# Four row transposes issued together, weight steps begun earlier, two products moved ahead of the last mixing

## The chip, the cores and the metric

One core of a Trainium2 chip runs the whole program. The metric is the device time of one execution in microseconds; of the kernel before there are three runs. The engines carry short names: PE is TensorE (PEld its weight loads), DVE is VectorE, ACT is ScalarE, POOL is GpSimd and SP is SyncE, which here only issues DMAs. SPq is SP's queue of DMA issues.

## The reference

Three stages follow one another. Gated linear attention over 4 batches, 8 heads, 768 positions and head size 48; a dense block on the 3072 tokens; a mixture of 8 experts in which each token goes to two.

```python
state = alpha[t][:, None] * state + outer(k[t], v[t]);  y[t] = q[t] @ state     # per batch and head
h = (x @ w1) * (x @ w2) @ w3;  x = h @ w_out                                     # 384 -> 1024 -> 384
top2 of x @ w_gate + log1p(exp(x @ w_noise)) * noise;  two weights by softmax
out[rows of expert e] += weight * (relu(x[rows] @ ew1[e]) @ ew2[e])              # 384 -> 1024 -> 384
```

## The kernel before, in words

**Chunks and groups.** Attention goes in 24 chunks of 128 tokens (j = 0 to 23). For each chunk PE runs `scores` (L293), `mix` (L326: four products of the queries with the running state `Zs`, L332, and 24 products of scores and values, L343), `state` (L354: the update of `Zs`, whose products are read and scaled on DVE at L386 and L387) and `xturn` (L389: six small transposes of the chunk's result). Three chunks are one group of 384 tokens (g = 0 to 7). The dense block runs by groups: 16 `wide` products per group (L516, nine matmuls each), then six `narrow` halves (L539, twelve matmuls each), then `finish` and `route` on DVE and ACT (L559, L597), which leave the two experts of each token and a one-hot count `M`. `rank` (L644) turns `M` into places in a table of tokens with two small matmuls (L650, L651), some DVE work, and six indirect DMAs on POOL. The rank of the last group is run inside `experts`.

**Who sets the order.** The order on PE is written by hand. `att_units` (L692) yields the attention steps with a planned cost each, `mix_units` (L790) the dense steps. After each attention step, as many dense steps are put behind it as the planned costs allow: the sum of dense costs may be 1.9 times the attention cost beyond 60. With these costs nothing is put between `xturn(22)` and `mix(23)`, the last mixing; four `wide` products of group 6, a rank and one `narrow` half stand between `mix(23)` and `xturn(23)`. When attention is over, the rest of `mix_units` follows, and after each unit of cost above zero `prepare(n)` (L1021) issues n steps of the list `todo`, with n from the tuple `EARLY`. On DVE, ACT, POOL and SP the order is chosen by the scheduler of the framework from the order in the program and from readiness, except that a step of `todo` stands behind the last DVE and ACT instructions issued so far, and that the DMAs sent through `queued` (L819) keep their order on each engine.

**Weights of an expert.** `expert_weights` (L830) gives two lists of steps: `a` for the first matrix (13 steps) and `b` for the second (11). In each: 0 and 1 load its halves (`get`, L856, 768 KB each, into one of three buffers `es`); 2 and 3 take the greatest absolute value of a half (DVE, L859; the second one ends in `em`, L862); 4 is empty; 5 is `over_all`, a PE matmul of one column (L867) that waits for `em`; 6 is `scales`; from 7 on the halves are cut into a high and a low f16 part (`eh` on ACT, L174, and `el` on DVE, L178), six cuts for `a`, four for `b`. A fourth half can be loaded when a buffer is free again, thus after the cuts of an earlier half.

**Experts.** An expert has 832 rows in two parts, 512 and 320. `fetch_part` loads the row numbers (`mt`, SP) and gathers the rows by indirect DMA (POOL, `xg`); `turn_part` (L966) transposes 128 rows by DMA into `xT` (SP, L894). Part 0 of all experts has one `xT` buffer. `first(e, p, f)` is one product of the first layer (L900 to L902, nine matmuls, evicted by ACT at L903 and DVE at L904), eight to a part; `second(e, p, t)` (L910 to L912, 24 matmuls) ends in a `put` of 128 rows (ACT L933, POOL L934). Expert 0's part 0 is followed by expert 1's part 0, then part 1 of both.

In `experts` before, expert 1's weight steps begin after the last `narrow` half. Its list has 24 entries, five of them empty: one is issued after each of the eight `first(0, 0, f)`, three after each `second(0, 0, t)`, one after each `first(1, 0, f)`. `rank(7)` comes after the eight `first`. Each of expert 1's four row transposes is issued ahead of its own `second(0, 0, t)`; the row numbers and gathers of expert 0's part 1 come after the first `second`.

Of the kernel before, what the change touches and what calls it, by code (L numbers as in the profile page):

```python
# [29 lines left out]
TG = G // P  # L30
NG = NTOK // G
# [22 lines left out]
RATIO = 2.0  # L54
TK = 60
R2 = 1.9
EARLY = (0, 3, 0, 3, 2, 1, 0, 1, 0, 1, 0, 1, 0, 1, 0, 0, 0, 0, 2, 0, 1, 1, 1, 1, 0, 0, 0, 0)
PGL = range(4)
NPC = 4
PB = 512  # L60
# [18 lines left out]
def body(ctx, tc, q, k, v, alpha, mw1, mw2, mw3, mwo, wg, wn, noise, ew1, ew2, out, dbg=None):  # L79
# [309 lines left out]
    def xturn(j):  # L389
        ys = YS.pop(j)  # L390
        if j % TG == 0:
            XT[j // TG] = xp.tile([P, 2 * NK, G], F16, name="xT")
        xt = bank(2 * NK, P, dt=F16)
        for kk in range(2 * NK):
            nc.tensor.transpose(xt[:, kk, :], ys[:, kk // NK, kk % NK * P:(kk % NK + 1) * P], ident16)
        nc.scalar.activation(XT[j // TG][:, :, j % TG * P:(j % TG + 1) * P], xt, AF.Copy)  # L396
# [292 lines left out]
    def unit(c, f, *a):  # L689
        return c, (lambda: f(*a))  # L690

    def att_units():  # L692
        yield unit(0.0, prep_open, 0)
        for pr in range(NP):
            yield unit(0.33, prep_decay, 0, pr)
            if pr:
                yield unit(0.66, prep_qk, 0, pr - 1)
        yield unit(0.66, prep_qk, 0, NP - 1)
        yield unit(1.7, scores, 0)
        yield unit(0.44, ktok, 0)  # L700
        yield unit(1.7, scores, 1)
        yield unit(2.55, mix, 0)
        yield unit(0.44, ktok, 1)
        yield unit(0.75, state, 0)
        yield 0.34, (lambda: (xturn(0), done.add(0)))
        yield unit(0.0, loads_of_1)
        yield unit(1.7, scores, 2)
        yield unit(2.55, mix, 1)
        yield unit(0.44, ktok, 2)
        yield unit(0.75, state, 1)  # L710
        yield 0.34, (lambda: (xturn(1), done.add(1)))
        yield unit(0.0, prep_open, 1)
        yield unit(0.0, norms, 1)
        yield unit(0.33, prep_decay, 1, 0)
        yield unit(2.55, mix, 2)
        yield unit(0.33, prep_decay, 1, 1)
        yield 0.34, (lambda: (xturn(2), done.add(2)))
        yield unit(0.66, prep_qk, 1, 0)
        yield unit(0.33, prep_decay, 1, 2)
        yield unit(0.66, prep_qk, 1, 1)  # L720
        yield unit(0.33, prep_decay, 1, 3)
        yield unit(0.66, prep_qk, 1, 2)
        yield unit(0.66, prep_qk, 1, 3)
        yield unit(0.0, scales_of, 1)
        yield unit(0.0, load, 2)
        yield unit(0.0, tables)
        yield unit(0.75, state, 2)
        yield unit(1.7, scores, 3)
        yield unit(0.44, ktok, 3)
        for j in range(TG, NG * TG):  # L730
            st, cc = divmod(j, TG)
            more = st + 1 < NG
            if j + 1 < NG * TG:
                yield unit(1.7, scores, j + 1)
            if more and cc == 0:
                yield unit(0.0, prep_open, st + 1)
                yield unit(0.0, norms, st + 1)
                yield unit(0.33, prep_decay, st + 1, 0)
                yield unit(0.33, prep_decay, st + 1, 1)
            yield unit(2.55, mix, j)  # L740
            if more and cc == 0:
                yield unit(0.66, prep_qk, st + 1, 0)
                yield unit(0.33, prep_decay, st + 1, 2)
            if more and cc == 1:
                yield unit(0.66, prep_qk, st + 1, 2)
            if j + 1 < NG * TG:
                yield unit(0.44, ktok, j + 1)
            yield unit(0.75, state, j)
            if more and cc == 0:
                yield unit(0.66, prep_qk, st + 1, 1)  # L750
                yield unit(0.33, prep_decay, st + 1, 3)
            if more and cc == 1:
                yield unit(0.66, prep_qk, st + 1, 3)
                yield unit(0.0, scales_of, st + 1)
                if st + 2 < NG:
                    yield unit(0.0, load, st + 2)
            yield 0.34, (lambda j=j: (xturn(j), done.add(j)))

    def fuse_units():

# [192 lines left out]
    NTP = [-(-(c1 - c0) // P) for c0, c1 in PARTS]  # L953
    EW, EX, EH, WV = {}, {}, {}, {}
    adds = {}
    todo = []

    def fetch_part(e, p):
        c0, c1 = PARTS[p]
        t0, nt = c0 // P, -(-(c1 - c0) // P)  # L960
        rows = P + NTOK - (NL * G if e < NFR and p == 0 else 0)
        mt = slots(table[e, :, t0:t0 + nt, :], nt, p)
        xT = ep.tile([P, 2 * NK, nt * P], F16, name=f"xT{p}", bufs=1)
        EX[e, p] = (mt, xT, [gather(mt, t, rows) for t in range(nt)])

    def turn_part(e, p, t):  # L966
        mt, xT, xg = EX[e, p]
        turn(xg[t], xT, t)
# [29 lines left out]
    def open_experts():  # L998
        nonlocal ep
        ep = ctx.enter_context(tc.tile_pool(name="ep", bufs=2, side="right", reuse_waits="tile"))  # L1000
        assert NG - NL not in RT and NG - NL - 1 not in RT
        a, b = weights_for(0)
        todo.extend(a[2:4] + b[2:3] + a[5:10] + b[1:2] + a[10:] + b[3:4] + b[5:])
        for e in range(NFR):
            fetch_part(e, 0)

    def weights_for(e):

        EW[e], a, b = expert_weights(e)
        for get in a[:2] + b[:1]:  # L1010
            get()
        return a, b

    def pause(n):
        return [lambda: None] * n
# [5 lines left out]
    def prepare(n):  # L1021

        if not n or not todo:
            return
        with ExitStack() as st:
            for e in (mybir.EngineType.DVE, mybir.EngineType.Activation):
                for i in [i for i in nc.cur_bb.bb.instructions[-60:] if i.engine == e][-1:]:
                    st.enter_context(tc.issue_after(i))
            for _ in range(min(n, len(todo))):
                todo.pop(0)()  # L1030

    def experts():
        prepare(len(todo))
        a, b = weights_for(1)
        todo.extend(pause(1) + a[2:4] + pause(1) + a[5:11] + b[1:2] + a[11:] + b[2:3] + pause(2) + b[3:4] + pause(1) + b[5:])
        for f in range(NF):
            first(0, 0, f)
            prepare(1)
        rank(NG - 1)
        for t in range(NTP[0]):  # L1040
            turn_part(1, 0, t)
            second(0, 0, t)
            prepare(3)
            if t == 0:
                fetch_part(0, 1)
        for f in range(NF):
            first(1, 0, f)
            prepare(1)
            if 0 < f <= NTP[1]:
                turn_part(0, 1, f - 1)  # L1050
        prepare(len(todo))
        fetch_part(1, 1)
        next_weights(2)
        for f in range(NF):
            first(0, 1, f)
            prepare(f // 4)
        for t in range(NTP[1] - 1):
            turn_part(1, 1, t)
            second(0, 1, t)
            prepare(2)  # L1060
        turn_part(1, 1, NTP[1] - 1)
        rest = last_few(0)
        li = overflow_plan()
        for e in range(1, E):
            if e > 1:
                for f in range(NF):
                    first(e, 0, f)
                    if f == 0:
                        rest()
                    prepare(1)  # L1070
            if e + 1 < E:
                fetch_part(e + 1, 0)
            for f in range(NF):
                first(e, 1, f)
                if f == 0 and e == 1:
                    rest()
                prepare(1)
            if e + 1 < E:
                fetch_part(e + 1, 1)
            for t in range(NTP[0]):  # L1080
                second(e, 0, t)
                prepare(2)
                if e + 1 < E:
                    turn_part(e + 1, 0, t)
            prepare(len(todo))
            if e + 2 < E:
                next_weights(e + 2)
            if e < E - 1:
                for t in range(NTP[1] - 1):
                    turn_part(e + 1, 1, t)  # L1090
                    second(e, 1, t)
                turn_part(e + 1, 1, NTP[1] - 1)
                rest = last_few(e)
        second(E - 1, 1, 0)
        rest = last_few(E - 1)
        second(E - 1, 1, 1, rest)
        return li
# [65 lines left out]
    done, ready = set(), set()  # L1163
# [3 lines left out]
    with tc.manual_schedule(engines={mybir.EngineType.PE}):  # L1167
# [4 lines left out]
        for c, f in att_units():  # L1172
# [16 lines left out]
            while nxt is not None and nxt[2] in ready | {0} and tm < RATIO * (min(ta, TK) - t0) + R2 * max(ta - TK, 0.0):  # L1189
                nxt[1]()  # L1190
                tm += nxt[0]
                nxt = next(M, None)
        att.close()
        open_experts()
        early = iter(EARLY)
        while nxt is not None:
# [38 lines left out]
```

## Time and profile before

| | us |
|---|---|
| median of three runs | 972.02 |
| lowest, highest | 971.38, 975.17 |
| the profiled execution itself | 978.31 |
| its span (first to last instruction) | 976.6 |
| PE busy | 924.2 (95%) |
| DVE, ACT, POOL busy | 616.1, 457.8, 254.0 |

The profiled execution is 6.29 us above the median of the runs; 1.71 us of it lie outside the span. Times in the rows are counted from the start of the span. In a row of a timeline stand start, duration, engine, line, operation, destination and sources, shapes, how often, and in square brackets the idle time of the engine before it with what ended it. A row that covers several instructions runs from the first start to the last end.

### The profile page before, as it was taken

The numbers are of one execution on the slowest core, as the hardware profiler recorded it, in microseconds if no ns is written. First come the engines' busy times: TensorE is split into PE (matmuls) and PEld (weight loads), VectorE is DVE, ScalarE is ACT, GpSimd is POOL, SyncE is SP. The second block draws the span as 40 slices with busy tenths as digits, with TensorE's granted clock in tenths as the row PEclk, the third lists the DMA queues.
The fourth block names the chain that finished last, engine by engine and source line by source line (L and its number), as shares of the span: only waits on it lengthen the run. The fifth ranks groups of instructions, "written<-read, shape, count | busy, mean of one in ns | idle before, by whom it ended". The sixth has DMA issues, their size and how long they took to land. (4 is left out here: it accounts for less than half of the span.)

```text
span 976.6 us, 17652 instructions
## 1 busy us (share of the span) xinstructions
PE 924.2 (95%) x6823; PEld 607.8 (62%) x6823; DVE 616.1 (63%) x1697; ACT 457.8 (47%) x916; POOL 254.0 (26%) x246
## 2 busy tenths in 40 slices
PE   7889999999899998999999989999999999999996
PEld 4777777777666675666655445654656565656564
DVE  6698878576778697686768736626354454545320
ACT  3876665363565746555446424324243343334321
POOL 1121110004041311204052061433333333333313
PEclk9798899999999999999999989999999999999998
DMA  9886571334805224000234264874658575656313
GB/s 242 224 163 109 162 195 53 63 52 145 187 3 96 27 66 58 25 2 26 68 102 127 87 129 139 138 174 104 167 89 163 102 178 118 161 124 157 41 13 46
DMA packets 189269, 105.54 MB, mean 108 GB/s; under 512 B 156912, under 2 KB 174912, under 8 KB 189184
## 3 DMA queue, kind: packets, MB, share of 16 engines
q1 hardware_dynamic: 172624, 68.04, 31.5%
q0 software_dynamic: 16560, 36.37, 17.3%
q8 instruction: 54, 0.88, 0.4%
q14 instruction: 31, 0.25, 0.1%
HBM read 73.06 MB, written 20.31 MB: 96 GB/s over the span
## 5 line engine op out<-in xcount | busy, mean ns | idle before, releaser
L904 DVE SCALAR_TENSOR_TENSOR hl<-ps,hh 128x512 f16<-128x512 f32 (+1 forms) x128 | 74.9, 587 | 110.9 <-ACT hh L903 110.9
L934 POOL DMA_INDIRECT out_dram<-ysb,mt x56 | 88.3, 1576 | 210.3 <-ACT ysb L933 91.3
L900 PE MATMUL ps<-xT,eh 128*128 128x320 f16 (+1 forms) x384 | 132.0, 344 | 4.5 <-DMA xT<-xg 4.5
L901 PE MATMUL ps<-xT,eh 128*128 128x320 f16 (+1 forms) x384 | 131.9, 344 | 0.0
L902 PE MATMUL ps<-xT,el 128*128 128x320 f16 (+1 forms) x384 | 131.7, 343 | 0.0
L912 PE MATMUL ps<-eh,hl 128*128 128x384 f16 x384 | 125.2, 326 | 0.0
L911 PE MATMUL ps<-el,hh 128*128 128x384 f16 x384 | 125.2, 326 | 0.0
L910 PE MATMUL ps<-eh,hh 128*128 128x384 f16 x384 | 125.2, 326 | 0.0
L903 ACT ACTIVATE hh<-ps 128x512 f16<-128x512 f32 (+1 forms) x128 | 65.9, 516 | 113.6 <-PE ps L902 112.5
L933 ACT ACTIVATE ysb<-ps,wv 128x384 f32<-128x384 f32 (+1 forms) x56 | 32.5, 580 | 151.9 <-PE ps L912 75.2
L178 DVE SCALAR_TENSOR_TENSOR el<-es,esc,eh 128x512 f16<-128x512 f32 (+1 forms) x80 | 67.0, 856 | 46.4 <-ACT eh L174 45.1
L679 POOL DMA_INDIRECT table<-md,ad x48 | 49.3, 1028 | 162.7 <-DVE ad L676 130.4
L888 POOL DMA_INDIRECT xg<-x2s,mt x56 | 56.4, 1008 | 57.8 <-DMA mt<-table 37.6
L176 POOL TENSOR_TENSOR sm<-sf,sm 128x512 f16<-128x512 f32 x24 | 28.4, 1203 | 161.1 <-ACT sm L174 161.1
L529 ACT ACTIVATE ab<-ps 128x384 f32<-128x384 f32 (+2 forms) x136 | 61.4, 465 | 17.0 <-PE ps L527 15.5
L525 PE MATMUL ps<-xT,w1h 128*128 128x384 f16 (+2 forms) x204 | 65.7, 323 | 2.0 <-ACT ab L529 1.5
L525 PE MATMUL ps<-xT,w0h 128*128 128x384 f16 (+2 forms) x204 | 65.4, 322 | 1.1 <-ACT xT L396 1.1
L549 PE MATMUL ps<-Wh,gh 128*128 128x400 f16 x192 | 63.9, 333 | 2.2 <-ACT gh L174 2.2
L527 PE MATMUL ps<-xT,w1l 128*128 128x384 f16 (+2 forms) x204 | 65.8, 323 | 0.0
L526 PE MATMUL ps<-xT,w1h 128*128 128x384 f16 (+2 forms) x204 | 65.7, 323 | 0.0
L526 PE MATMUL ps<-xT,w0h 128*128 128x384 f16 (+2 forms) x204 | 65.4, 322 | 0.0
L527 PE MATMUL ps<-xT,w0l 128*128 128x384 f16 (+2 forms) x204 | 65.3, 321 | 0.0
(285 smaller groups left out, 2080.6 us busy)
## 6 DMA issues: line engine op xcount, KB each, us to landing
es<-in_moe_w_dram SPq DMA_DIRECT2D x32, 768.0 KB, 4.8
s<-in_moe_w_dram POOLq DMA_DIRECT2D x16, 512.0 KB, 4.3
out_dram<-zero POOLq DMA_DIRECT2D x5, 960.0 KB, 9.4
v<-in_v_dram SPq DMA_DIRECT2D x24, 192.0 KB, 3.6
x2s<-xr SPq DMA_DIRECT2D x24, 192.0 KB, 1.9
pad<-in_alpha_dram SPq DMA_DIRECT2D x21, 192.0 KB, 4.3
pad<-in_q_dram SPq DMA_DIRECT2D x21, 192.0 KB, 4.8
pad<-in_k_dram SPq DMA_DIRECT2D x21, 192.0 KB, 5.0
```

The lines of the kernel that those rows point to most:

```text
L178: nc.vector.scalar_tensor_tensor(lo, src, scale, hi, op0=OP.mult, op1=OP.subtract)
L525: nc.tensor.matmul(pm, wab[i][0][:, kk, fs], xT[:, kk, cs], start=kk == 0, stop=False)
L526: nc.tensor.matmul(pm, wab[i][0][:, kk, fs], xT[:, NK + kk, cs], start=False, stop=False)
L527: nc.tensor.matmul(pm, wab[i][1][:, kk, fs], xT[:, kk, cs], start=False, stop=kk == NK - 1)
L900: nc.tensor.matmul(pm, w1h[:, kk, fs], xT[:, kk, :n], start=kk == 0, stop=False)
L901: nc.tensor.matmul(pm, w1h[:, kk, fs], xT[:, NK + kk, :n], start=False, stop=False)
L902: nc.tensor.matmul(pm, w1l[:, kk, fs], xT[:, kk, :n], start=False, stop=kk == NK - 1)
L904: nc.vector.scalar_tensor_tensor(hl[:, f], pm, 0.0, hh[:, f], op0=OP.max, op1=OP.subtract)
L910: nc.tensor.matmul(py[:n], hh[:, f, ts], w2h[:, f], start=f == 0, stop=False)
L911: nc.tensor.matmul(py[:n], hh[:, f, ts], w2l[:, f], start=False, stop=False)
L912: nc.tensor.matmul(py[:n], hl[:, f, ts], w2h[:, f], start=False, stop=f == NF - 1)
L934: i = queued(lambda: nc.gpsimd.indirect_dma_start(out=out, out_offset=bass.IndirectOffsetOnAxis(ap=mt[:n, t, 0:1].bitcast(U32), axis=0), i ...
```

## The change

Four things change. The planned cost of `mix(23)` falls by 1.6 and that of `xturn(22)` rises by 1.6, so two `wide` products and `rank(5)` are put between them. In `EARLY`, three steps of expert 0 are issued one or two units sooner, after `narrow(6, 2, 0)`, and two steps of expert 1 are issued after `narrow(7, 1, 0)` and `narrow(7, 2, 0)`. Expert 1's list has no empty entries, and the load of the second half of its second matrix, `b[1]`, stands ahead of the cuts. In `experts`, the four transposes are issued together, ahead of `rank(7)`, and two steps in place of three follow each `second(0, 0, t)`. The number of matmuls, cuts, loads and transposes stays the same.

```diff
-EARLY = (0, 3, 0, 3, 2, 1, 0, 1, 0, 1, 0, 1, 0, 1, 0, 0, 0, 0, 2, 0, 1, 1, 1, 1, 0, 0, 0, 0)
+MH = 1.6
+EARLY = (0, 3, 0, 6, 0, 0, 0, 1, 0, 1, 0, 1, 0, 1, 0, 0, 0, 0, 2, 0, 1, 1, 1, 1, 1, 0, 1, 0)
...
-            yield unit(2.55, mix, j)
+            yield unit(2.55 - (MH if j == NG * TG - 1 else 0.0), mix, j)
...
-            yield 0.34, (lambda j=j: (xturn(j), done.add(j)))
+            late_on = MH if j == NG * TG - 2 else 0.0
+            yield 0.34 + late_on, (lambda j=j: (xturn(j), done.add(j)))
...
+        todo.append(first_of_1)
+
+    def first_of_1():
+        a, b = weights_for(1)
+        todo.extend(a[2:4] + a[5:7] + [b[1]] + a[7:11] + [b[2]] + a[11:] + b[3:4] + b[5:])
+        todo.pop(0)()
...
     def experts():
-        prepare(len(todo))
-        a, b = weights_for(1)
-        todo.extend(pause(1) + a[2:4] + pause(1) + a[5:11] + b[1:2] + a[11:] + b[2:3] + pause(2) + b[3:4] + pause(1) + b[5:])
         for f in range(NF):
             first(0, 0, f)
-            prepare(1)
+            prepare((0, 1, 1, 1, 1, 1, 1, 1)[f])
+        for t in range(NTP[0]):
+            turn_part(1, 0, t)
         rank(NG - 1)
         for t in range(NTP[0]):
-            turn_part(1, 0, t)
             second(0, 0, t)
-            prepare(3)
+            prepare(2)
             if t == 0:
                 fetch_part(0, 1)
```

## Rows read from the trace of the kernel before

**Rows 1.** The profile page, busy time and share of PE.

```profile
PE 924.2 (95%) x6823; PEld 607.8 (62%) x6823; DVE 616.1 (63%) x1697; ACT 457.8 (47%) x916; POOL 254.0 (26%) x246
```

**Rows 2.** Waits of PE from 470 to 600 us: total, times, longest.

```profile
PE ps L900 <- DMA xT<-xg: 4.5, 1, 4.5
PE ps L867 <- DVE em L862: 3.2, 2, 1.6
PE ps L332 <- DVE Zs L387: 2.0, 1, 2.0
PE ps L651 <- DVE M L640: 0.5, 1, 0.5
```

**Rows 3.** Waits of PE from 600 us to the end.

```profile
PE ps L867 <- DVE em L862: 3.2, 5, 2.4
```

**Rows 4.** Timeline of PE about the last two mixings.

```profile
470.50 1.03 PE L332 MATMUL ps<-Zs,Qt 112*128 112x96 f32 x8
...
473.44 0.33 PE L525 MATMUL ps<-xT,w0h 128*128 128x384 f16 x1
...
482.56 1.57 PE L332 MATMUL ps<-Zs,Qt 112*128 112x96 f32 x8 [2.00 <-DVE Zs L387]
...
487.12 0.33 PE L525 MATMUL ps<-xT,w1h 128*128 128x384 f16 x1
```

**Rows 5.** Windows: length, busy PE, PEld, DVE, ACT, POOL, granted clock, DMA, GB/s.

```profile
484.00:486.00 2.00, 2.00 (x29) 1.48 (x28) 0.38 (x4) 0.58 (x2) 0.00 (x0) 0.50 0.41 33
544.00:559.00 15.00, 13.40 (x64) 5.90 (x63) 14.55 (x63) 5.63 (x12) 0.00 (x0) 1.00 0.11 40
580.00:582.00 2.00, 2.00 (x5) 0.66 (x6) 0.00 (x0) 0.00 (x0) 1.70 (x2) 0.50 1.07 176
```

**Rows 6.** Timeline of DVE about the last two mixings.

```profile
476.73 0.62 DVE L178 SCALAR_TENSOR_TENSOR ys<-ps,xsc,ys 128x384 f16<-128x384 f32 x1 [0.65 <-ACT ys L174]
...
481.67 0.74 DVE L387 TENSOR_TENSOR Zs<-Zs,Ae 48x192 f32<-48x192 f32 x2
```

**Rows 7.** Timeline of DVE about the early weight steps.

```profile
522.61 1.75 DVE L859 TENSOR_REDUCE esc<-es 128x1 f32<-128x1536 f32 x1 [0.32 <-DMA es<-in_moe_w_dram]
...
542.52 0.17 DVE L169 TENSOR_SCALAR am<-am 128x3 int32<-128x3 int32 x1 [5.44 <-ACT xr L554]
...
558.79 0.75 DVE L178 SCALAR_TENSOR_TENSOR el<-es,esc,eh 128x512 f16<-128x512 f32 x1
...
574.04 0.29 DVE L949 TENSOR_SCALAR wv<-mt,esc,esc 128x3 f32<-128x3 f32 x1 [1.64 <-DMA mt<-table]
574.24 0.15 DVE L862 TENSOR_REDUCE em<-esc 128x1 bf16<-128x2 f32 x1
```

**Rows 8.** Timeline of SP's DMA queue, 510 to 600 us.

```profile
517.93 0.38 SPq L856 DMA_DIRECT2D es<-in_moe_w_dram  x1
518.37 5.72 SPq L894 DMA_TRANSPOSE xT<-xg  x4
524.19 13.29 SPq L856 DMA_DIRECT2D es<-in_moe_w_dram  x3
...
565.80 0.39 SPq L856 DMA_DIRECT2D es<-in_moe_w_dram  x1
...
572.77 10.90 SPq L894 DMA_TRANSPOSE xT<-xg  x6
```

**Rows 9.** Timeline of PE, experts 0 and 1, 559 to 600 us.

```profile
559.67 0.17 PE L651 MATMUL ps<-M,ones 128*128 128x24 bf16 x1 [0.50 <-DVE M L640]
...
579.97 0.58 PE L900 MATMUL ps<-xT,eh 128*128 128x512 f16 x1 [4.51 <-DMA xT<-xg]
...
585.04 0.58 PE L900 MATMUL ps<-xT,eh 128*128 128x512 f16 x1
...
598.19 0.30 PE L900 MATMUL ps<-xT,eh 128*128 128x320 f16 x1
```

**Rows 10.** Instructions that touch the tile xT: DMA time from issue to landing.

```profile
DMA to landing us min/median/max: 2.8/4.5/8.7
```

## The prediction

> **What bounds the kernel now.** I read the busy table first. PE is busy for 95% of the span, the next engine for 63% [rows 1]: the time is PE's work plus PE's waits, and an edit pays where it takes a wait of PE away. So the second view is the waits of PE, cut at 600 us, because the change touches the stretch from the last mixing to expert 1's first products. In that stretch PE waits four ways, 10.2 us in all [rows 2]: 4.5 for expert 1's transposed rows, 3.2 in two waits of 1.6 each for `em`, 2.0 for the state `Zs`, 0.5 for the counts `M`. From 600 us on there are 3.2 us for `em` [rows 3], about which the change does nothing.
>
> The third view is the granted clock by windows. A wait can cost more than its length. The window 484 to 486 is at 0.50, and so is 580 to 582: 1.2 GHz in place of 2.4 [rows 5]. Both lie right behind the 2.0 us and the 4.5 us wait. Behind the 1.6 us waits I saw no such stretch: 544 to 559, which holds one of them, is at 1.00 [rows 5]. The same row shows DVE busy for 14.55 of 15 us; there the next wait can come from.
>
> **The change part by part.**
>
> *Last mixing.* In the profile `mix(23)` starts at 482.56, after 2.00 us in which `Zs` is awaited; from its start to the end of the first product behind it 4.56 us pass (482.56 to 487.12). The same two items at `mix(22)` take 2.94 us (470.50 to 473.44) [rows 4]; the difference, 1.62 us, is the slow clock. DVE writes `Zs` from 481.67 for 0.74 us, so to 482.41 [rows 6]. After the change two `wide` products stand here. An estimate of one: twelve matmuls of 512 columns take 5.07 us at 1.2 GHz [rows 9], 0.41 ns a column at 2.4 GHz, so nine of 384 columns take 1.43 us. Two fill 480.56 to 483.42, past 482.41 with 1.0 us to spare. Gain 2.0 + 1.6 = 3.6 us. The price lies behind the mixing: its result must go through ACT and DVE before `xturn(23)`, and two products less cover that. Two products and one `narrow` half stay, 1.43 + 1.43 + 2.0 (twelve matmuls of 400 columns by the same estimate) = 4.9 us. For `mix(22)` the last DVE step ended at 477.35 [rows 6], 5.4 us after the mixing ended near 472.0 (473.44 [rows 4] less one product). So the cost is between 0 and 0.5 us; I take 0, because the last mixing has no scores of a next chunk beside it, and keep 0.5 for the range.
>
> *Expert 0's steps.* The load of its fourth half is issued at 517.93 [rows 8] and DVE waits 0.32 us for its landing before the reduction of 1.75 us at 522.61 [rows 7]; `em` follows, and PE's first 1.6 us wait is for it. The change issues the two cuts before it and the load one or two units sooner. A unit is a `narrow` half or a product, 2.0 or 1.5 us, so up to 3.5 us, more than 1.6. Gain 1.6 us. The three moved steps add no instruction; what they are moved past is `finish` of group 6 on DVE and ACT and its three stores on SP, which nobody awaits for 10 us. Bounds 0 and 1.6.
>
> *Expert 1's first steps.* Its two reductions, 1.75 us each, stand now among the routing of group 7 on the saturated DVE; the second wait for `em` is behind them. In the change they follow `narrow(7, 1, 0)` and `narrow(7, 2, 0)`, where DVE idles 5.44 us ahead of 542.52 [rows 7], room for 3.5 us. The loads do not move: they are issued from 524.19 to 537.48 [rows 8] already, ahead of their place in the program, because they wait for free buffers. Gain 1.6 us. Bounds 0 and 1.6.
>
> *Counts.* `rank(7)` still stands behind the eight `first` on PE, and its wait depends on DVE, which is full from 542.52 until `M`. It loses two reductions (3.5 us) and gets about three cuts more (three times 0.75 [rows 7]), so `M` is ready 1.3 us sooner; PE comes 1.6 us sooner. The wait of 0.5 becomes about 0.8. Bounds: 0 to 2.0. I take a loss of 0.2 with the scheduler's freedom in mind.
>
> *Transposes.* Now one transpose goes ahead, the last three in the group of six from 572.77 [rows 8]; PE stands from 575.46 to 579.97 and then runs at 1.2 GHz: twelve matmuls take 5.07 us, 579.97 to 585.04 [rows 9]. At 2.4 GHz they take half, so 2.5 us are clock. After the change the four are queued together once `first(0, 0, 7)` has read `xT`, about 559.2 (559.67 less the wait of 0.50 [rows 9]). Four took 5.72 us of SP's queue [rows 8], and a landing takes 4.5 us, at most 8.7 [rows 10]: the rows are there by 559.2 + 5.7 + 4.5 = 569.4, at worst 573.6, and PE needs them at 575.5. Gain 4.5 + 2.5 = 7.0 us. What is late next are expert 0's own three transposes for its second part; they were issued last in that group, by 583.67, and PE needs them at 598.19 [rows 9], 7.0 us sooner after the change: 7.5 us are left, and a landing takes 4.5.
>
> *Waits added on a queue.* On SP the load `b[1]` now stands ahead of the four transposes and waits for the third cut of the first matrix; if that cut is late, four transposes are late with it (a rival, below).
>
> **Sum.** 3.6 + 1.6 + 1.6 - 0.2 + 7.0 = 13.6 us, of which 4.1 are clock and 9.5 are waits. Against the profiled execution: 978.31 - 13.6 = 964.7. The runs without a profile have a median 6.29 us lower, and nothing shows which of the stalls they have as long; I keep the 9.5 and take 2.5 of the 4.1: 972.02 - 12.0 = 960.0 us. What a measurement of this kernel can tell from no change is about 0.5%, 4.9 us.
>
> **The rivals.**
>
> *A wait in place of the one removed, on DVE.* In the profile `em` at 574.24 stands right behind `wv` at 574.04, which sat 1.64 us until the row numbers `mt` had landed [rows 7]: a small instruction that waits for a DMA holds the reduction's result behind it. The Trainium skill says the same of the engine (TensorE: Matmul & The Clock Gate, section "Part 1: The HAM clock gate"): VectorE and ScalarE run strictly first in, first out; by that rule too the order on DVE, not readiness, decides here. The change moves `over_all` of expert 1's second matrix from after the fourth to after the third `second`, 3.9 us sooner (four `second` fill 559.67 to 575.46 [rows 9]; about 571.5), while `mt` comes when it came, because it waits for the table that `rank(7)` writes. If `wv` is put ahead of `em` again, PE waits until 574.4, 2.9 us, long enough for the clock to fall as behind the 2.0 us wait, so 2.5 more: 12.0 - 5.5 = 6.5 us gained, 965.5. For: the order of before. Against: the reduction is issued one step sooner. 0.09.
>
> *The transposes stay late.* The change then doesn't do what it says: SP stands at `b[1]`. That load was issued at 565.80 before [rows 8]; at the same moment it would put the four transposes at 566.2 to 571.9, landed at 576.4, 1 us late. With the cut 2 us later still, the wait is 3 us and the clock falls: again 6.5 us gained, 965.5. Against: cuts are issued one by one from the fifth `first`, about 4 us sooner than before. 0.09.
>
> *Given back later.* PE reaches the later experts sooner and waits there for `put` and `em`. For it: five `em` waits [rows 3]. Against: they are 3.2 us together, and their partners are released by PE's own progress, so they move along. To eat the gain they would have to grow fourfold: 971. 0.07.
>
> *Slower.* Expert 1's second reduction stands on DVE ahead of `finish` of group 7, and waits for a load that SP issues as the second of the three from 524.19 [rows 8], when a buffer is free. DVE idles until 542.52, and the load of before was out by 537. If it lands later than about 540.8 (542.52 less 1.75), all of `route` is late by as much, then `M`, then PE at `rank(7)`, one for one, and from 2 us on the clock falls too. It decides only from far: the loss must pass 12 + 4.9 us, thus a load near 555. In the profile nothing holds SP that long there, but that order is the scheduler's. 978 or more. 0.05.
>
> **How the numbers follow.** The forecast has 0.70, all of it faster by over 0.5%. The two rivals at 965.5 lie 6.5 us below the median, near the bound of 4.9; I count half of each as faster. Faster: 0.70 + 0.045 + 0.045 = 0.79. Same: 0.045 + 0.045 + 0.07 = 0.16. Slower: 0.05. The range: at the low end 13.6 us, the 0.5 and 0.2 of `M` not lost, and 2.2 of the later waits gone, 16.5: 955.5. At the high end the rivals at 965.5 with half of an `em` wait and 0.7 of `M` left, 967.0. What is left out is the part given back and the slower case, 0.12, and tails.
>
> **What would show it.** In the changed profile: `mix(23)` with no wait on `Zs` and no window below 1.00 between 480 and 490; no wait for `em` before 600 us; four transposes in one row of SP's queue near 555; no wait of L900 for `xT`. Wrong it would be with PE waiting 2 us or more at L651 or L867, with `xturn(23)` waiting for `ys`, or with the em waits after 600 us grown well beyond 3.2.

## The result and the profile after

The changed kernel takes 966.41 us (median of 20 runs), the kernel before, run on the same chip, 975.26 us (20 runs): 0.9911 of the time, 95% interval 0.9895 to 0.9926, a gain of 8.9 us. I had forecast 960.0, a gain of 12.0. So the absolute miss of 6.4 us has two halves: 3.2 us because the three runs shown stood below the median of twenty (972.02 against 975.26), and 3.2 us because the gain was smaller. The result stands 0.6 us inside the upper end of my range (955.5 to 967.0), an end that I had built from rivals that did not come; that it holds is in part luck.

The busy table of the profile after, the line that answers to [rows 1]. The profiled execution took 966.37 us, its span is 964.6.

```profile
PE 918.4 (95%) x6823; PEld 604.2 (63%) x6823; DVE 615.6 (64%) x1697; ACT 457.3 (47%) x916; POOL 254.0 (26%) x246
```

PE is busy for 5.8 us less with the same 6823 matmuls: they run at 2.4 GHz for longer (the mean granted clock of the two profiled executions is 0.973 of it before and 0.981 after). The rest of the 12.0 us between the spans is waits. The waits of PE in the kernel after from 470 to 600 us, to hold against [rows 2]:

```profile
PE ps L652 <- DVE M L641: 1.6, 1, 1.6
PE ps L651 <- DVE M L639: 1.0, 1, 1.0
PE ps L902 <- DVE hl L906: 0.8, 1, 0.8
```

And its waits from 600 us to the end, against [rows 3]:

```profile
PE ps L869 <- DVE em L864: 1.3, 5, 0.6
```

All four kinds of wait of [rows 2] are gone: for `Zs`, for `xT`, twice for `em`, for `M` at `rank(7)`. But 2.6 us at `rank(6)` are new (L651 and L652 are `rank` after the change, one line further down than before), and 0.8 for the `hl` of expert 1. Windows of the kernel after (columns as in [rows 5]) show what the first two do to the clock:

```profile
482.00:484.00 2.00, 2.00 (x14) 1.20 (x13) 1.87 (x6) 1.12 (x3) 0.00 (x0) 1.00 0.00 0
484.00:486.00 2.00, 2.00 (x29) 1.70 (x27) 1.38 (x7) 1.28 (x3) 0.00 (x0) 1.00 0.00 0
486.00:488.00 2.00, 2.00 (x31) 1.35 (x27) 1.90 (x12) 0.99 (x3) 0.00 (x0) 1.00 0.27 51
...
522.00:524.00 2.00, 1.73 (x7) 0.88 (x7) 1.79 (x11) 0.52 (x1) 0.00 (x0) 0.51 1.06 409
524.00:526.00 2.00, 2.00 (x11) 0.97 (x10) 1.54 (x10) 0.49 (x1) 0.60 (x1) 0.64 0.03 9
```

Around the last mixing, where one window stood at 0.50 [rows 5], the granted clock is 1.00 throughout; behind `rank(6)` it now falls to 0.51 and 0.64. The change took a stall away in one place and made one in another.

One profile against one profile says little here. Up to `xturn(22)` all kernels of this document run the same instructions, and yet its start lies between 477.38 us (e4) and 487.08 (e9) in the profiles. So the kernel before was profiled a second time, and the table below goes by stages, over fourteen profiles. Each number is the distance between two starts on PE's timeline: of `xturn(22)` and `xturn(23)` (mixing); from there to expert 0's first product (groups 6 and 7); from there to expert 1's first product (expert 0); from there to the first product of expert 0's part 1 (expert 1); and from there to the end. "M" is the time from ACT's last eviction of group 6 (the last L554 or L555 ahead of the exponentials) to the start of DVE's first write of `M` for `rank(6)`. "M less idle" is the same without the time in which DVE stood idle between the exponentials and `M` (the square brackets of its timeline). Where steps of expert 0 stand early, a star is set.

| kernel | mixing | groups 6, 7 | expert 0 | expert 1 | to the end | M | M less idle |
|---|---|---|---|---|---|---|---|
| before | 13.55 | 48.04 | 38.32 | 18.22 | 378.41 | 13.48 | 13.5 |
| before, second profile | 13.60 | 52.11 | 38.33 | 18.07 | 375.33 | 15.96 | 13.6 |
| mixing alone (e1) | 9.84 | 51.97 | 38.30 | 17.72 | 373.95 | 17.42 | 13.7 |
| transposes alone (e2) | 13.56 | 54.36 | 33.67 | 15.54 | 373.79 | 18.19 | 13.6 |
| mixing and transposes (e9) | 9.84 | 53.53 | 33.68 | 15.54 | 374.53 | 17.32 | 13.6 |
| steps alone (e3)* | 13.56 | 53.06 | 36.65 | 18.12 | 373.92 | 20.16 | 17.2 |
| after* | 9.84 | 50.60 | 31.24 | 16.51 | 374.98 | 17.85 | 17.1 |
| after, second profile* | 9.84 | 53.33 | 31.24 | 16.51 | 378.46 | 19.44 | 16.9 |
| expert 0's steps undone (e5) | 9.85 | 53.12 | 31.24 | 15.54 | 374.11 | 17.29 | 13.7 |
| reduction later (e6)* | 9.85 | 52.83 | 31.25 | 17.40 | 374.43 | 19.63 | 15.6 |
| rank(6) later (e4)* | 9.85 | 50.98 | 31.24 | 16.48 | 375.07 | 21.02 | 17.0 |
| rank(6) later, steps undone (e11) | 9.85 | 49.29 | 31.24 | 15.54 | 380.14 | 15.19 | 13.6 |
| rank(6) later still (e12)* | 9.85 | 50.19 | 31.90 | 17.65 | 375.01 | 21.53 | 17.1 |
| rank(6) and reduction later (e10)* | 9.84 | 56.28 | 31.24 | 17.03 | 376.23 | 19.45 | 15.5 |

Three of the stages repeat to within 0.2 us between the two executions of before and the two of after: mixing, expert 0, expert 1. "Groups 6, 7" and "to the end" scatter by some 4 us within one kernel (48.04 and 52.11 before), so single profiles decide nothing there.

### The profile page after: what moved, and what is told of

It is laid out like the page before. It is cut to its first block, busy times and chain, and to the rows that moved or that the text cites. A ratio compares the mean times of both kernels' runs of the same rounds, so it can differ in the third digit from the quotient of the medians.

```text
span 964.6 us, 17647 instructions
## 1 busy us (share of the span) xinstructions
PE 918.4 (95%) x6823; PEld 604.2 (63%) x6823; DVE 615.6 (64%) x1697; ACT 457.3 (47%) x916; POOL 254.0 (26%) x246
## 4 chain that ended last, share of the span: by engine, by line
PE 57%; DVE 21%; ACT 7%; issue 6%; DMA 4%; SPq 2%; POOL 1%; POOLq 0%; ACTq 0%; DVEq 0%
PE ps L912 6%; PE ps L913 6%; PE ps L914 6%; PE ps L902 5%; PE ps L904 5%; PE ps L903 5%; PE ps L526 2%; PE ps L528 2%; PE ps L527 2%; PE ps L552 2%; PE ps L550 2%; PE ps L551 2%; DVE esc L861 2%; PE ps L344 2%; DVE Gx L230 2%
## 5 line engine op out<-in xcount | busy, mean ns | idle before, releaser
L902 PE MATMUL ps<-xT,eh 128*128 128x320 f16 (+1 forms) x384 | 130.2, 339 | 1.1 <-DVE hl L906 0.8
L903 PE MATMUL ps<-xT,eh 128*128 128x320 f16 (+1 forms) x384 | 130.2, 339 | 0.0
```

The lines of the kernel that those rows point to most:

```text
L902: nc.tensor.matmul(pm, w1h[:, kk, fs], xT[:, kk, :n], start=kk == 0, stop=False)
L903: nc.tensor.matmul(pm, w1h[:, kk, fs], xT[:, NK + kk, :n], start=False, stop=False)
```

## The experiments

**One part at a time.** Four kernels, made from the kernel before (e1, e2, e9) or after (e3), ran together against 34 runs of before (979.7 us on that chip).

e1_mix, the planned costs alone:

```diff
+MH = 1.6
-            yield unit(2.55, mix, j)
+            yield unit(2.55 - (MH if j == NG * TG - 1 else 0.0), mix, j)
-            yield 0.34, (lambda j=j: (xturn(j), done.add(j)))
+            late_on = MH if j == NG * TG - 2 else 0.0
+            yield 0.34 + late_on, (lambda j=j: (xturn(j), done.add(j)))
```

> The planned costs alone are changed: two wide products and rank(5) stand between xturn(22) and mix(23). If the prediction's first term holds by itself, PE has no wait for Zs, no window below 1.00 between 480 and 490 us, and the stretch from xturn(22) to xturn(23) is about 3.6 us shorter in the profile (13.55 us before); in the timed runs 2.0 to 3.6 us less than before, a ratio of 0.996 to 0.998. If the cover that was taken from behind the last mixing was needed, xturn(23) waits for ys by 1 us or more and the ratio is 1.000.

Measured: 977.48 us, 0.9961 (0.9932 to 0.999). The mixing stage falls from 13.6 to 9.84 us. Expert 0 stays where it was, and expert 1 is 0.4 to 0.5 us shorter.

e2_turns, the transposes alone:

```diff
+        for t in range(NTP[0]):
+            turn_part(1, 0, t)
         rank(NG - 1)
         for t in range(NTP[0]):
-            turn_part(1, 0, t)
             second(0, 0, t)
```

> Expert 1's four transposes alone are issued together, ahead of rank(7); weight steps as before. If the fifth term holds by itself, the wait of L900 for xT and the stretch at 1.2 GHz behind it are gone: 7.0 us less in the profile, 4.5 to 7.0 in the timed runs, a ratio of 0.993 to 0.9955. If the wait only passes on to the next thing that is late (em behind wv, or expert 0's second part), PE waits there for 2 us or more and the ratio is above 0.997.

Measured: 975.81 us, 0.9952 (0.9918 to 0.9987). Expert 0 falls by 4.65 us (the wait), expert 1 by 2.5 to 2.7 (the clock behind it): 7.2 us in the profile. The timed runs show 3.9 by the medians, within an interval of 1.3 to 8.

e3_steps, the kernel after with the two others undone, so the weight steps alone:

```diff
-MH = 1.6
+MH = 0.0
-        for t in range(NTP[0]):
-            turn_part(1, 0, t)
         rank(NG - 1)
         for t in range(NTP[0]):
+            turn_part(1, 0, t)
             second(0, 0, t)
```

> The weight steps alone are changed; the planned costs and the place of the transposes are those of before. By the profile of the changed kernel (2.6 us of waits at rank(6), then a slow clock, in place of the em wait of 1.6; the em wait of expert 1 gone) the steps are worth about nothing: a ratio of 0.998 to 1.002. By the prediction's second and third terms they are worth 3.2 us: a ratio of 0.9965 or below.

Measured: 979.59 us, 0.9998 (0.9968 to 1.0027): nothing clear of an interval of 3 us to either side. PE's waits from 470 to 600 us in e3 say why:

```profile
PE ps L902 <- DMA xT<-xg: 5.3, 1, 5.3
PE ps L651 <- DVE M L639: 2.7, 1, 2.7
PE ps L333 <- DVE Zs L388: 2.0, 1, 2.0
PE ps L652 <- DVE M L641: 1.6, 1, 1.6
```

No `em` is waited for any more, as meant, but `M` is, for 4.3 us at `rank(6)`.

e9_mixturns, the edits of e1 and e2 together:

> The planned costs and the four transposes together are changed; weight steps as before. If the steps are worth nothing, this kernel is as fast as the changed one: a ratio near 0.991. If they are worth the 3.2 us of the prediction, it is slower than the changed one by that: near 0.9945. The two em waits of 1.6 us stay in its profile either way.

Measured: 972.79 us, 0.9919 (0.9885 to 0.9954). That is the whole change (0.9911) without its weight steps, and close to the product of the two parts, 0.9961 times 0.9952 = 0.9913. The interval takes in the 0.9945 of the other expectation too; it is e3 that speaks against a gain of 3.2 us, which would be 0.9967, just outside its interval. The two `em` waits stay, but with 3.6 and 1.6 us. **The gain comes from the mixing and the transposes; the weight steps, taken together, bring none that these runs can tell.**

**Where the weight steps' gain went.** The next four kernels ran together against 11 runs of before (979.04 us).

c_after, the changed kernel again:

> The changed kernel once more, unaltered, as the measure for the three kernels that run beside it. Both theories: 0.991 of the time before (0.988 to 0.994), and in the profile PE waits at rank(6) for the counts M in two waits, 1.0 and 1.6 us in the one profile so far, with the clock at 0.51 and 0.64 in the two windows behind them; no wait for em before 600 us, none for Zs, none for xT.

Measured: 970.15 us, 0.9901 (0.9879 to 0.9923). The waits for `M` are there in the second profile too. Its waits of PE from 470 to 600 us, the first two:

```profile
PE ps L651 <- DVE M L639: 2.6, 1, 2.6
PE ps L652 <- DVE M L641: 1.6, 1, 1.6
```

e5_early, expert 0's three steps back in their old places, the rest as after:

```diff
-EARLY = (0, 3, 0, 6, 0, 0, 0, 1, 0, 1, 0, 1, 0, 1, 0, 0, 0, 0, 2, 0, 1, 1, 1, 1, 1, 0, 1, 0)
+EARLY = (0, 3, 0, 3, 2, 1, 0, 1, 0, 1, 0, 1, 0, 1, 0, 0, 0, 0, 2, 0, 1, 1, 1, 1, 1, 0, 1, 0)
```

> The changed kernel with expert 0's last three weight steps (cut, cut, load) given back to their old places in the order: one part of the change undone. Order theory: the reduction stands behind M on DVE again, so the waits at rank(6) shrink from 2.6 us to at most 1.1, and a wait for em of 1.6 to 3.6 us at over_all comes back; the two are worth the same, so the time is within 1.5 us of the changed kernel. My prediction's step (the steps gain 1.6 us and cost nothing): 1.6 us slower than the changed kernel. Load theory: within 1.5 us too, and the waits add up to as much as in the changed kernel.

Measured: 968.19 us, 0.9879 (0.9856 to 0.9903). It is not slower by 1.6 us, as my step said, but 2 us faster by the medians, which the intervals don't separate. PE's waits in e5 from 470 to 600 us:

```profile
PE ps L869 <- DVE em L864: 3.5, 1, 3.5
PE ps L652 <- DVE M L641: 1.1, 1, 1.1
PE ps L651 <- DVE M L639: 0.3, 1, 0.3
```

The wait has changed its place: 3.5 for `em` at `over_all` and 1.4 for `M` here, against 4.2 for `M` and none for `em` in the profile taken beside it.

e6_reduce tells two reasons apart. In the profile after, expert 0's last reduction (1.74 us) stands on DVE ahead of `M`, since its load lands sooner; before, it stood behind `M`, at 522.61 [rows 7]. DVE's timeline in the kernel after:

```profile
518.40 1.74 DVE L861 TENSOR_REDUCE esc<-es 128x1 f32<-128x1536 f32 x1
520.06 0.17 DVE L624 TENSOR_TENSOR oh<-rev,rr 128x24 f32<-128x24 f32 x1
520.15 0.17 DVE L632 RECIPROCAL w<-w 128x3 f32<-128x3 f32 x1
520.24 0.13 DVE L864 TENSOR_REDUCE em<-esc 128x1 bf16<-128x2 f32 x1
520.28 0.17 DVE L639 TENSOR_TENSOR M<-oh 128x24 bf16<-128x24 f32 x1
```

The edit puts the reduction, `over_all` and the scales further back and leaves the cuts early:

```diff
-EARLY = (0, 3, 0, 6, 0, 0, 0, 1, 0, 1, 0, 1, 0, 1, 0, 0, 0, 0, 2, 0, 1, 1, 1, 1, 1, 0, 1, 0)
+EARLY = (0, 3, 0, 6, 0, 0, 0, 1, 0, 1, 0, 1, 0, 0, 0, 0, 0, 1, 0, 0, 3, 1, 1, 1, 1, 0, 1, 0)
```

> The changed kernel with expert 0's last reduction put behind rank(6)'s counts on DVE, and over_all and the scales behind it two places further back; cuts and loads stay early. Order theory: M is ready 1.7 us sooner, the waits at rank(6) shrink from 2.6 us to under 1 us and the clock stays up, no wait for em takes their place because over_all is later too: 2.5 to 4 us faster than the changed kernel beside it, 0.996 to 0.9975 of it. Load theory (the three moved cuts of 2.07 us and the late third store of the turned rows hold DVE, not the reduction): 1 to 2 us of the waits at rank(6) stay, and the time is within 1.5 us of the changed kernel.

Measured: 968.04 us, 0.9893 (0.9864 to 0.9921). The reduction went behind `M`, as DVE's timeline in e6 shows:

```profile
520.78 0.18 DVE L639 TENSOR_TENSOR M<-oh 128x24 bf16<-128x24 f32 x1
...
526.22 1.75 DVE L861 TENSOR_REDUCE esc<-es 128x1 f32<-128x1536 f32 x1
```

and PE waited for `M` all the same, 2.4 and 0.8 us. Read alone, that says that the reduction does not matter. But on the way to `M` DVE stood idle for 4.04 us in this execution, against 2.53 and 0.76 in the two profiles of after. DVE's timeline in e6:

```profile
511.47 0.56 DVE L177 TENSOR_TENSOR gl<-ab,gh 128x384 f16<-128x384 f32 x1 [4.04 <-ACT gh L175]
```

ACT had stood still itself (last section), a thing that comes and goes between executions. The column "M" mixes this with the change. With expert 0's steps in their old places it runs from 13.5 to 18.2 us (seven profiles, mean 16.4), with all of them early from 17.9 to 21.5 (five, mean 20.0). "M less idle" falls into three groups instead: 13.5 to 13.7 us with the steps in their old places, 15.5 and 15.6 with the cuts early and the reduction behind `M` (e10, e6), 16.9 to 17.2 with both early. Within a group the numbers differ by 0.3 us at most, so the idle time is not part of what the edits do, as far as this shows. So both theories were half right: **the reduction holds `M` up by some 1.5 us, the early cuts (with the load) by some 2.0.** By this estimate e6 without its idle time would have had `M` at 15.6 us, and PE comes to `rank(6)` some 17 us after the same eviction. In the timed runs e6 is 2 us faster than the changed kernel by the medians, within the intervals.

How the cuts do it, ACT shows. They stand on ACT and DVE between the last eviction of group 6 and all that follows from it. ACT's timeline in the first profile of the kernel before:

```profile
504.77 0.19 ACT L554 ACTIVATION_READ_ACCUMULATOR xr<-ps 128x1 f32 x1
504.86 0.71 ACT L174 ACTIVATE eh<-es,esc 128x512 f16<-128x512 f32 x1
...
506.87 0.21 ACT L605 ACTIVATE ex<-x 128x24 f32<-128x24 f32 x1
```

The same stretch of ACT's timeline in the kernel after:

```profile
502.43 0.19 ACT L555 ACTIVATION_READ_ACCUMULATOR xr<-ps 128x1 f32 x1
502.53 1.94 ACT L175 ACTIVATE eh<-es,esc 128x512 f16<-128x512 f32 x3
...
505.76 0.21 ACT L606 ACTIVATE ex<-x 128x24 f32<-128x24 f32 x1
```

Three cuts instead of one: the exponentials, with which the routing begins, start 3.33 us after the last eviction instead of 2.10. That 1.2 is the same in each of the fourteen profiles (3.32 or 3.33 with the star, 2.10 or 2.11 without). The other 0.8 of the 2.0 lies further down, where DVE has done six cuts by `M` in place of four; it was not taken apart. In e6 and e10 the load stays early along with the cuts, so no run separates these two.

e4_rank6 asks the other way round: leave `M` late and let PE ask for it later.

```diff
-RF = 5
+RF = 6
```

This puts `rank(6)` behind two more `wide` products, some 2.9 us of PE's work. (The expectation calls that one narrow product and has `over_all` move along; in the trace `over_all` keeps its place and now stands just ahead of `rank(6)`. Where the expectations of e10, e11 and e12 count one product or two, it is two and four.)

> The changed kernel with rank(6) one narrow product further back in PE's order (over_all of expert 0's second matrix moves back by a product with it). Order theory (M is late because expert 0's last reduction, 1.74 us, now stands ahead of it on DVE): PE has one product, 1.5 to 2.0 us, more to do before it asks for M, so of the two waits of 2.6 us in all under 1 us is left and the clock stays at 1.00 there, 2 to 4 us faster than the changed kernel beside it, 0.996 to 0.998 of it. Load theory (DVE has more to do in this stretch than PE and any wait taken away comes back at the next place): the wait moves to em or to first of expert 0, and the time stays within 1 us of the changed kernel. Third theory (the reader is PE in order, and the cost of this stretch lies in the profiled execution alone): the same time, and no wait in either profile.

Measured: 965.58 us, 0.9864 (0.9838 to 0.989), 4.6 us under the changed kernel beside it. PE's waits in e4 from 470 to 600 us, the first three:

```profile
PE ps L652 <- DVE M L641: 1.6, 1, 1.6
PE ps L902 <- DVE hl L906: 0.8, 1, 0.8
PE ps L869 <- DVE em L864: 0.7, 1, 0.7
```

The wait at L651 is gone, 0.7 for `em` came, and the 1.6 at L652 stay; the clock still falls behind them (last section). The gain over before is 13.5 us by the medians, about the 12.0 that I had forecast for the change, and five of the six runs lie below the fastest of the changed kernel beside it. So in the timed runs a later `rank(6)` pays. **Where it pays is not shown:** e4's profile takes 483.6 us from `xturn(22)` to its end, as the first profile of after does (483.2), and starts that stretch 4 us sooner, out of instructions that are the same in both. PE's timeline in e4, to hold against 481.43 in the kernel after (next section):

```profile
477.38 0.50 PE L396 MATMUL ps<-ident,ys 128*128 128x128 f16 x6
```

Against the second profile of after it is 5.8 us shorter there, of which 2.4 lie in groups 6 and 7 and 3.4 after expert 1.

**Can more be had?** The last four ran against 11 runs of before (979.2 us).

c_before, the kernel before:

> The kernel before, unaltered, for a second profile. If the waits that my prediction read are those of the kernel and not of one execution: Zs 2.0 us and xT 4.5 us again, within 0.5. Of the em waits before 600 us and of rank(6) I expect other sizes than in the first profile: the three kernels that leave expert 0's steps alone showed 3.5 us for em at expert 0's over_all and 1.1 us for M at rank(6), against 1.6 and 0. If the 2.38 us wait for em at 666.7 belongs to one execution, it is under 1 us here.

One run, 984.71 us. PE's waits in this second profile of the kernel before, from 470 to 600 us:

```profile
PE ps L867 <- DVE em L862: 5.1, 2, 3.5
PE ps L900 <- DMA xT<-xg: 4.5, 1, 4.5
PE ps L332 <- DVE Zs L387: 2.0, 1, 2.0
PE ps L651 <- DVE M L640: 0.9, 2, 0.5
```

`Zs` and `xT` repeat to the tenth. `em` at expert 0's `over_all` does not: 3.5 us where [rows 2] had 1.6. The 2.38 us for `em` at 666.6 us in the first profile are 0.6 here.

e11_r6early, `RF = 6` with the `EARLY` of e5:

> The changed kernel with rank(6) one product further back and expert 0's last three weight steps in their old places. Order theory: with M out of the way, the moved steps are worth what I gave them in the prediction, so giving them back costs an em wait of 1.6 to 3.5 us and its slow clock: 0.988 to 0.990 of the time before, 1.6 to 4 us slower than the product alone. Load theory: the steps are worth nothing with or without the product, ratio 0.986 to 0.987.

Measured: 968.35 us, 0.9898 (0.9865 to 0.9931). Above e4 by the point, not separated from it: the point lies where the order theory put it, the interval takes in both. PE waits 1.9 us for `em` and not for `M`.

e12_rank7, `RF = 7`:

> The changed kernel with rank(6) two products further back. Order theory: no wait for M is left at rank(6), where one product alone left 1.6 us; over_all is one more product later too, so no em wait: 1 to 2 us faster than one product, 0.984 to 0.986 of the time before, as long as expert 0's rows, which hang on rank(6), still come in time; if they do not, PE waits for xT at the first product of expert 0 and the time is 0.988 or more. Load theory: 0.986 to 0.987, waits moved to later places.

Measured: 967.4 us, 0.9896 (0.9864 to 0.9927), above what either theory had for rows that come in time. The wait for `M` at `rank(6)` is gone, and others came: 1.9 for `hl`, 1.6 for `gh`.

e10_both, `RF = 6` with the reduction behind `M`:

> The changed kernel with rank(6) one product further back and expert 0's last reduction behind rank(6)'s counts on DVE as well. Order theory: the waits at rank(6) are gone (under 0.5 us, where one product alone left 1.6), 1 to 2.5 us faster than with the product alone, 0.984 to 0.986 of the time before. Load theory (ACT and DVE of this stretch, not PE's place in it, set the end): the time saved at rank(6) is waited for at over_all or at the hl of expert 1, and the ratio is that of the product alone, 0.986 to 0.987.

Measured: 972.06 us, 0.993 (0.9902 to 0.9958), a miss for both theories. I moved the reduction too far: DVE starts it at 529.66, and PE stands at `over_all` for 6.5 us, the longest wait met here.

So e4 has the lowest ratio to the kernel before. That it beats e5, e11 or e12 is not shown, and the lowest of several such points is in part picked by chance.

## Why the prediction was right, and where it was wrong

**Last mixing: right.** Predicted 3.6 us; the stage takes 9.84 or 9.85 us in every profile with the edit, against 13.55 to 13.60 in every one without, 3.7 less. `mix(23)` starts after `xturn(22)`, two products and `rank(5)`, with no wait. The price of up to 0.5 us that I kept in the range did not appear. PE's timeline in the kernel after:

```profile
481.43 0.50 PE L396 MATMUL ps<-ident,ys 128*128 128x128 f16 x6
...
484.77 1.11 PE L333 MATMUL ps<-Zs,Qt 112*128 112x96 f32 x8
```

**Transposes: right.** Predicted 4.5 us of wait and 2.5 of clock; alone they brought 4.65 and 2.5 to 2.7. SP's queue in the kernel after, against [rows 8]:

```profile
558.95 0.38 SPq L858 DMA_DIRECT2D es<-in_moe_w_dram  x1
559.43 5.69 SPq L896 DMA_TRANSPOSE xT<-xg  x4
...
577.39 4.35 SPq L896 DMA_TRANSPOSE xT<-xg  x3
```

The four begin at 559.43 (I had 559.2) and PE starts expert 1 at 573.11 without a wait.

**Expert 1's first steps and the counts: right, a little small.** Predicted 1.6 less 0.2; expert 0's stage is 33.67 us with the transposes alone and 31.24 with the steps too, 2.4 less. The second `em` wait (1.6) went, and the 0.5 at `rank(7)` went as well instead of growing.

**Expert 0's steps: the step that failed.** I gave them 1.6 us, with the bounds 0 and 1.6, on the ground that "what they are moved past is `finish` of group 6 on DVE and ACT and its three stores on SP, which nobody awaits for 10 us". That is true of `finish` itself and false of what follows from it. From the eviction ahead of `finish` a chain runs through the exponentials, the logarithm and the two choices of an expert to `M`, and PE asks for `M` at `rank(6)`. In the first profile before, DVE stood idle nowhere on that chain; the part of `M` for which PE's second product waits was written at 519.59, and PE came at 521.67, so there were 2 us to spare. DVE's and PE's timelines in the first profile of the kernel before:

```profile
518.25 0.18 DVE L638 TENSOR_TENSOR M<-oh 128x24 bf16<-128x24 f32 x1
...
519.59 0.16 DVE L640 CAST M<-R 128x8 bf16<-128x8 f32 x1
```

```profile
521.67 0.18 PE L650 MATMUL ps<-M,before 128*128 128x24 bf16 x1
```

In the second none were left, PE waited 0.4. I had read when `finish` was done and not the end of its chain. I had also mis-sized the move: the load, which I let go up to 3.5 us sooner, was issued 13.2 us after the last eviction of group 6 in the first profile before (517.93 [rows 8], 504.77) and 3.0 us after it in the kernel after. SP's queue there:

```profile
505.48 0.38 SPq L858 DMA_DIRECT2D es<-in_moe_w_dram  x1
```

With its load there that early the reduction, of which the term says nothing, came ahead of `M`. Cuts and reduction together make `M` 3.5 us later ("M less idle", 13.6 to 17.1), PE waits 2.6 to 4.3 us at `rank(6)`, and the clock falls. Against that stands a real gain larger than mine: the `em` wait that went was 3.5 us in the other profiles. As far as the runs can tell, the two cancel: e5 against c_after is 2 us within the intervals, and the stage "groups 6, 7" takes 52.2 us with the steps in their old places and 52.3 with them early (means of six profiles and of three, with `rank(6)` and the reduction unmoved). My list of wrong signs had this one, a wait of 2 us or more at `rank`, but no rival named it, and the lower bound of the term should have been negative.

They cost a second time. In both profiles of the change the `hl` of expert 1 is awaited for 0.8 us and its stage takes 16.51 us; with the steps in their old places (e5, e11) it takes 15.54. That was not traced to its cause.

**The sum.** Predicted for the profile: 13.6. The mean of the two profiles before, less that of the two after, gives 3.7 for the mixing, -1.9 for groups 6 and 7 (50.08 to 51.97), 7.1 for expert 0, 1.6 for expert 1, 0.2 for the end: 10.7. Against my terms that is 0.1 more, 3.5 less, 1.2 more and 0.9 less, with 0.2 at the end; the 3.5 is uncertain, since that stage scatters by 4 us, and by the means just given it would be 1.7. The timed runs show 8.9. My cut from 13.6 to 12.0 for runs without a profile went the right way for the wrong reason: it took something off the clock, where a whole term was missing. That the forecast came near is luck to that extent.

**The rivals.** The order on DVE did not turn against the change at `wv`, as the first rival had it (it did at `M`, where no rival stood), and the transposes were not held up by `b[1]`, which was issued 0.5 us ahead of them (above). DVE's timeline in the kernel after, about `wv`:

```profile
565.49 0.16 DVE L864 TENSOR_REDUCE em<-esc 128x1 bf16<-128x2 f32 x1
...
572.51 0.29 DVE L951 TENSOR_SCALAR wv<-mt,esc,esc 128x3 f32<-128x3 f32 x1 [5.05 <-DMA mt<-table]
```

`wv` sat 5.05 us for `mt`, longer than before, but `em` was ahead of it. The rule that I had set beside this rival (the Trainium skill, TensorE: Matmul & The Clock Gate, section "Part 1: The HAM clock gate": VectorE and ScalarE run strictly first in, first out) bears on a place where I had not applied it: the trace agrees, two more cuts in front of the routing made all of it 1.2 us late on ACT. The slower rival came within sight: DVE did wait for a load ahead of `finish(7)`, 1.16 us, and `finish` began right behind it, at 543.14. DVE's timeline in the kernel after:

```profile
541.47 1.75 DVE L861 TENSOR_REDUCE esc<-es 128x1 f32<-128x1536 f32 x1 [1.16 <-DMA es<-in_moe_w_dram]
543.14 0.16 DVE L170 TENSOR_SCALAR am<-am 128x3 int32<-128x3 int32 x1
```

It cost nothing, since `rank(7)` shows no wait. Nothing was given back after 600 us either: 376.9 us before and 376.7 after, as means of two profiles each, in a stage that scatters by 4 us.

## What to carry to other kernels

Work moved ahead on an in-order engine delays everything behind it there, so follow what it is moved past to the end of its chain and ask how long before PE's request that end comes; that the next instruction is awaited by nobody says nothing. Before a wait of one profile is made a term of a sum, take a second profile: the waits for `Zs` and `xT` came back to the tenth (2.0, 4.5), while one for `em` was 1.6 and 3.5. When the end of a chain moves between executions, take off the idle time of its engine before two kernels are compared: the raw column hid that the reduction mattered. When a result can't come sooner, let the reader ask later: two products between made the timed runs 4.6 us faster by the medians here.

## What was not expected of the hardware

**ACT stands still for nothing that the trace shows.** Behind the exponentials of group 6 ACT evicts `wide` products, and in most profiles one of these evictions starts late. ACT's timeline in e6:

```profile
504.58 0.86 ACT L530 ACTIVATE ab<-ps 128x384 f32<-128x384 f32 x2
509.93 0.49 ACT L530 ACTIVATE ab<-ps 128x384 f32<-128x384 f32 x1 [4.49 <-PE ps L528]
```

The product it names ended on PE at 505.05, and PE went on with the next. ACT's idle time ahead of such evictions comes to 4.0 us in e4, 4.5 in e6 and in the second profile of before, 5.4 in e9, and to 0.9 and 0.8 in the first profiles of before and after. DVE then waits for ACT and `M` is late: DVE's idle time is all but 0.2 us of the scatter of "M" between kernels with the steps in their old places, and 2.4 of the 4.1 us by which "groups 6, 7" differs between the two profiles of before. One suspect is the loading of instructions. The Trainium skill (Runtime: NRT & Kernel Launch, section "Instruction fetch mechanics") says that an engine streams its program by DMA in blocks and that this is mostly hidden. In e4, e6 and e9 a packet of the queue that the profile calls "instruction" starts within 0.4 us of ACT's restart (in e4 and e6 just behind it), in e2, e3 and e5 1 to 2.4 us ahead of it. No run here tested it; it stays open.

**Behind two short waits in a row the clock fell as behind one long.** A single wait of 1.6 us left it at 1.00 [rows 5], in the second profile of before too, and so did the 1.9 us in e11. In the profile after, 1.0 and 1.6 us with 0.2 us of work between them brought 0.51; in e4, 0.7 and 1.6 us with 0.3 between brought 0.50. A window of e4:

```profile
522.00:524.00 2.00, 2.00 (x8) 0.91 (x6) 1.38 (x5) 1.28 (x3) 0.00 (x0) 0.50 0.00 0
```

A sum that prices waits one by one misses that.
